# A new order for the first two batches of a fused attention and gated-MLP kernel, with 35 casts and copies on other engines

## The chip, the cores and the metric

The kernel runs on one core of a Trainium2 chip. The core has a matrix engine (PE in the profile, with its weight loads as PEld), a vector engine (DVE), a scalar engine (ACT), a general engine (POOL) and an engine that here only issues transfers (SP). Each works through its own instructions strictly in the order of the program, and they wait for each other through semaphores. Data lie in main memory, in the on-chip memory, and in accumulation banks that PE writes and DVE and ACT read. The metric is the device time of one execution in microseconds (us); lower is better.

## The reference, cut to what matters

```
# q, k, v: [8 batches, 8 heads, 576 tokens, 64]
scores = q @ k^T / sqrt(64)
keep   = (0 <= i - j) and (i - j < 64)          # sliding causal window
attn   = softmax(where(keep, scores, -1e9)) @ v
x = attn, heads side by side                     # [8, 576, 512]

h = relu(x @ w_in)                               # w_in [512, 1024]
u, v = h[..., :512], h[..., 512:]
v_n = (v - mean(v)) / sqrt(var(v) + 1e-6)        # over the last axis
v_s = w_spatial @ v_n + b_spatial                # mixes the 576 tokens
out = (u * v_s) @ w_out                          # w_out [512, 512], float32
```

## The kernel before, in words

The code first makes a list of named steps, each with what it computes and what it needs. One long string, `ORDER`, then says in which order the steps are emitted, on which engine each runs, and which numbered buffer or bank it takes. A word such as `ck1_1:POOL:2` reads: step ck1_1, on POOL, into buffer 2. What stands earlier in the string for the same engine is executed earlier. Nothing else decides the order, and a buffer or bank that is taken again is waited for.

The names follow a scheme. The first digit is the batch (0 to 7). For attention the next is the half g (heads 0 to 3, or 4 to 7), and a third digit u is a pair of heads of that half; `r` in place of them is the last 64 tokens, all heads. For the gated MLP the digit behind the underscore is one of five blocks of tokens (or of features for U and G), and block 4 is the one of 64 tokens.

- `ldq`, `ldk`, `ldv`, `ldwin`, `ldwsp`, `ldwo`, `ldb`: loads, issued by SP in order (L401, L422, L327, L343, L384, L352). A q or k load brings one half (576 KB). A v load brings one block of 128 tokens (128 KB) in 256-byte pieces, five for a half. `ldwin100` to `ldwin111` are the four blocks of w_in for the V product (first digit 1), `ldwin000` to `ldwin011` those for U.
- `cq`, `ck`: casts to 16 bits. `tq`, `tk`: transposes on DVE (L408). `cv`, `sl`, `su`, `s4`: cast of v and copies of it shifted by half a block. `cwin`, `cwsp`, `cwo`, `cb`: casts of the weights. On ACT such a copy is at L293, elsewhere at L301, and long ones on POOL are cut into three at L296.
- `S`: scores on PE (L470, for `r` L539) into two pairs of banks. `E`: exponential on ACT (L477, L549). `M`: the mask, a minimum on DVE (L480, L553). `Z`: sums by a product with ones (L493, L562). `N`, `n`: logarithm and exponential of its negative, which gives the inverse (L519, L521). `P`: product with v (L504, L575). `X`: P times the inverse on DVE (L512, L583), which is x.
- `V`: x times the second half of w_in (L653; block 4 at L666). `Vr`: relu (L633). `Vb`, `Va`: statistics on DVE (L635, L637). `L1`, `L2`: inverse deviation on ACT (L680, L682). `A`: normalisation on DVE (L692). `U`, `Ur`: the other half and its relu (L708, L713, L721).
- `W`: transposes of w_spatial on PE (L368), copied out by `We`. `G`: the spatial product (L738; block 4 at L744). It needs all five A and all five We, and the bias. `Ge`: times u on DVE (L752). `O`, `Oe`, `st`: the output product (L763), its copy on ACT (L610) and the store. From batch 1 on, V of block 4 shares its bank with the output of block 4 of the batch before, so `V1_4` needs w_out and Ge0_4 as well.
- `D`: 25 steps of two products of zeros (L791), which keep PE busy in the first microseconds and compute nothing.

The batches overlap: while the MLP of one batch runs, the attention of the next is computed and the loads of later ones are issued. Loads of q, k and weights go through eight buffers of one kind (`nat`), those of v through four (`natv`); a load into a buffer waits until the casts of what lay there are done.

Of the kernel before, what the change touches and what calls it, by code (L numbers as in the profile page):

```python
# [47 lines left out]
Ge0_4:DVE:1 tq2_0:DVE:3 cv1_11:POOL ldq3_0:DQ:0 G0_1:PE:0 ldv2_00:DQ:0 s41_1:POOL sl1_11:ACT
su1_11:POOL n1_r:ACT Ge0_2:DVE:2 P1_10:PE:2 n1_11:ACT X1_10:DVE:3 ck2_1:POOL:2 P1_11:PE:1
ldk3_0:DQ:2 S2_0:PE:1:0 X1_11:DVE cwo10:ACT ldv2_01:DQ P1_r:PE:2 Ge0_0:DVE:3 V1_2:PE:1 E2_00:ACT:0  # L50
X1_r:DVE:1 Ge0_1:DVE:4 E2_01:ACT:1 V1_1:PE:3 cq2_1:POOL:3 ldv2_02:DQ tk2_1:DVE:0 V1_3:PE:2
Vr1_2:ACT:5 ldv2_03:DQ cwo00:POOL Vr1_1:ACT:6 tq2_1:DVE:1 U1_2:PE:0 ldv2_10:DQ:1 Vr1_3:ACT:7
cwo11:ACT ldv2_11:DQ V1_0:PE:1 M2_00:DVE Ur1_2:ACT:5 Vb1_2:DVE:5 cwo01:ACT S2_1:PE:1:0 Vr1_0:ACT:4
M2_01:DVE Z2_00:PE:3 cq3_0:POOL:0 ldv2_04:DQ E2_10:ACT:3 V1_4:PE:2 Vb1_1:DVE:1 ldv2_12:DQ Va1_2:DVE
Vb1_3:DVE:3 U1_1:PE:0 Vr1_4:ACT:2 M2_10:DVE Oe0_4:ACT:0 O0_0:PE:1 ck3_0:POOL:1 ldv2_13:DQ
Vb1_4:DVE:0 E2_11:ACT:2 Vb1_0:DVE:2 ldq4_0:DQ:3 O0_2:PE:2 Oe0_0:ACT:0 Va1_3:DVE ldv2_14:DQ Va1_4:DVE
Va1_1:DVE Ur1_1:ACT:0 Va1_0:DVE S2_r:PE:1:0 M2_11:DVE Z2_10:PE:1 cv2_00:POOL:1 ldv3_00:DQ:2
L11:ACT:1 O0_1:PE:0 tq3_0:DVE:4 L21:ACT Oe0_2:ACT:1 ldq3_1:DQ:1 N2_10:ACT:3 U1_4:PE:2 ldk3_1:DQ:4
A1_4:DVE E2_r0:ACT:0 U1_0:PE:1 N2_00:ACT:5 A1_0:DVE:4 ldv5_10:DQ:3 A1_2:DVE:5 Ur1_4:ACT:3 A1_1:DVE:6
U1_3:PE:3 Oe0_1:ACT A1_3:DVE:7 sl2_00:ACT:0 su2_00:POOL tk3_0:DVE:5 G1_1:PE:2 Ur1_3:ACT:1  # L60
cv2_10:POOL:0 Ur1_0:ACT:4 G1_0:PE:0 Ge1_1:DVE:5 n2_00:ACT sl2_10:POOL:1 s42_0:ACT Z2_01:PE:3
E2_r1:ACT ldv3_10:DQ:0 Ge1_0:DVE:6 s42_1:ACT P2_00:PE:1 Z2_11:PE:2 su2_10:POOL ldv3_11:DQ
N2_01:ACT:2 S3_0:PE:1:0 X2_00:DVE:0 ldv3_12:DQ N2_11:ACT:4 M2_r:DVE ldq4_1:DQ:7 P2_01:PE:0 n2_10:ACT
cq3_1:POOL:2 P2_10:PE:3 ldv3_13:DQ P2_11:PE:1 n2_11:ACT ldk4_0:DQ:5 X2_10:DVE:1 G1_3:PE:2
E3_00:ACT:0 X2_11:DVE cq4_0:POOL:3 ldv3_01:DQ G1_4:PE:3 n2_01:ACT Ge1_3:DVE:7 O0_3:PE:1 ck3_1:ACT:0
X2_01:DVE Ge1_4:DVE:8 Z2_r:PE:2 V2_2:PE:0 tq3_1:DVE:0 N2_r:ACT:1 E3_01:ACT:1 V2_0:PE:3 M3_01:DVE
V2_3:PE:2 Vr2_0:ACT:3 M3_00:DVE cq4_1:POOL:1 Vr2_2:ACT:1 U2_2:PE:3 tk3_1:DVE:1 Vr2_3:ACT:0 n2_r:ACT
V2_1:PE:0 cv3_10:POOL:2 Oe0_3:ACT Vb2_0:DVE:4 P2_r:PE:2 st0_1:DQ Vr2_1:ACT:2 Z3_00:PE:1 X2_r:DVE:0
S3_1:PE:1:0 sl3_10:POOL:2 st0_4:DQ N3_00:ACT:0 Vb2_3:DVE:5 ldv3_02:DQ U2_0:PE:0 Ur2_2:ACT:2
tq4_1:DVE:2 su3_10:POOL ldv3_03:DQ E3_10:ACT:3 ldv3_14:DQ G1_2:PE:2 ldv3_04:DQ ck4_0:POOL:2  # L70
tq4_0:DVE:3 E3_11:ACT:2 st0_0:DQ Z3_01:PE:1 V2_4:PE:3 Ur2_0:ACT:0 Vb2_1:DVE:3 N3_01:ACT:5 M3_10:DVE
S3_r:PE:1:0 Vr2_4:ACT:4 U2_4:PE:0 Ge1_2:DVE:9 E3_r0:ACT:1 U2_3:PE:1 E3_r1:ACT Va2_0:DVE M3_11:DVE
Ur2_4:ACT:4 cv3_00:POOL:3 Oe1_4:ACT:0 O1_2:PE:2 Vb2_2:DVE:0 n3_01:ACT st1_4:DQ Va2_3:DVE Vb2_4:DVE:1
O1_3:PE:0 n3_00:ACT ldk4_1:DQ:6 sl3_00:POOL:3 ldv4_00:DQ:1 Oe1_2:ACT:1 Va2_4:DVE Va2_2:DVE Va2_1:DVE
U2_1:PE:3 tk4_0:DVE:0 Ur2_3:ACT:1 su3_00:POOL L12:ACT:0 O1_0:PE:2 L22:ACT Oe1_3:ACT A2_4:DVE
s43_0:POOL A2_1:DVE:0 Ur2_1:ACT:3 O1_1:PE:1 ldv4_10:DQ:2 A2_3:DVE:1 s43_1:ACT ldk5_0:DQ:0 A2_0:DVE:2
Oe1_0:ACT:0 Z3_10:PE:0 A2_2:DVE:3 ldv4_11:DQ P3_00:PE:3 N3_10:ACT:3 P3_10:PE:2 ldq5_0:DQ:2
# [764 lines left out]
```

## Time and profile before

| what | value |
|---|---|
| time, median of 3 runs | 202.31 us (201.81 to 206.53) |
| profiled execution, span from first to last instruction | 201.0 us |
| PE busy | 188.6 us, 94% |
| DVE busy | 161.2 us, 80% |
| ACT busy | 167.0 us, 83% |
| POOL busy | 76.5 us, 38% |
| data moved | 42.69 MB, mean 212 GB/s |

The profile gives the profiled execution's time as its span, 201.0 us; the runs' times hold in addition what lies around the span, and their median is 1.3 us above it. Busy PE time counts matmuls as long as they are in the pipeline, so it is not PE at its peak. In the row of a group, the first two numbers are the start and the length in microseconds, xN the number of instructions, and what stands in brackets is the idle time of the engine before it and what ended it. In the chain of work that ended last there is only a start and a length. In a row of transfers the last number is the time from issue to landing.

### The profile page before, as it was taken

How to read it: one execution, taken by the hardware profiler on the slowest of the kernel's cores; microseconds unless marked ns; L12 is line 12 of the kernel's file. 1: busy time of each engine (PE TensorE's matmuls, PEld its weight loads, DVE VectorE, ACT ScalarE, POOL GpSimd, SP SyncE). 2: the span in 40 equal slices, each digit the busy share in tenths (PEclk: the TensorE clock that was granted, in tenths of full speed). 3: DMA queues.
4: the chain of work that ended last, by engine and by line, in shares of the span. 5: the costliest groups of instructions: out<-in, count | busy, mean ns of one | idle time of the engine just before them, and what ended most of it. 6: DMA issues, size and time to landing. Idle time of an engine off the chain costs nothing.

```text
span 201.0 us, 7008 instructions
## 1 busy us (share of the span) xinstructions
PE 188.6 (94%) x2927; PEld 97.7 (49%) x2927; DVE 161.2 (80%) x307; ACT 167.0 (83%) x307; POOL 76.5 (38%) x144
## 2 busy tenths in 40 slices
PE   7588889899999999989999999999999999999992
PEld 2233535545445445654455545554465455444450
...
GB/s 221 387 276 184 336 378 210 292 372 377 185 274 255 246 221 188 295 243 234 311 118 262 241 316 178 227 284 249 185 111 117 3 5 132 108 0 0 128 145 202
DMA packets 50275, 42.69 MB, mean 212 GB/s; under 512 B 39361, under 2 KB 39489, under 8 KB 50242
## 3 DMA queue, kind: packets, MB, share of 16 engines
...
q8 instruction: 23, 0.38, 0.8%
...
q14 instruction: 10, 0.08, 0.1%
...
## 4 chain that ended last, share of the span: by engine, by line
PE 70%; DMA 9%; SPq 7%; ACT 5%; DVE 5%; POOL 1%; issue 1%; POOLq 0%
PE bank L738 16%; PE bank L653 12%; PE bank L763 12%; PE bank L708 10%; DMA nk<-in_k_dram 9%; SPq L422 4%; PE pair L470 4%; PE bank L504 3%; PE bank L666 3%; PE bank L493 3%; PE bank L744 2%; SPq L327 2%; ACT e L477 1%; PE bank L713 1%; ACT ob L610 1%
## 5 line engine op out<-in xcount | busy, mean ns | idle before, releaser
L738 PE MATMUL bank<-wspT,vn 128*128 128x512 f16 (+1 forms) x160 | 37.5, 379 | 0.0
L477 ACT ACTIVATE e<-pair 128x1024 f16<-128x1024 f32 x32 | 31.9, 1027 | 2.7 <-PE pair L470 2.5
L752 DVE TENSOR_TENSOR g<-bank,ru 128x512 f16<-128x512 f32 (+1 forms) x40 | 24.8, 632 | 11.0 <-PE bank L738 5.0
L708 PE MATMUL bank<-x,win 128*128 128x512 f16 x128 | 31.6, 379 | 0.0
L763 PE MATMUL bank<-wout,g 128*128 128x512 f16 x128 | 31.3, 379 | 0.0
L653 PE MATMUL bank<-win,x 128*128 128x512 f16 x128 | 30.4, 379 | 0.2 <-DVE x L512 0.2
L721 ACT ACTIVATE ru<-bank 128x512 f32<-128x512 f32 (+1 forms) x40 | 21.4, 562 | 8.4 <-PE bank L708 4.6
L635 DVE BATCH_NORM_STATS2 st<-vs 128x6 f32<-128x512 f16 (+1 forms) x40 | 25.9, 670 | 3.0 <-ACT vs L633 2.8
L512 DVE TENSOR_TENSOR x<-bank,lz 128x512 f16<-128x512 f32 x32 | 21.2, 683 | 5.4 <-PE bank L504 2.6
L633 ACT ACTIVATE vs<-bank 128x512 f16<-128x512 f32 (+1 forms) x40 | 22.9, 597 | 3.1 <-PE bank L653 2.3
L610 ACT COPY ob<-bank 128x512 f32<-128x512 f32 (+1 forms) x39 | 22.6, 588 | 3.3 <-PE bank L763 3.1
L738 PEld LDWEIGHTS <-vn 128*128 128x128 f16 (+1 forms) x160 | 14.9, 97 | 17.7 <-DVE vn L692 0.5
L480 DVE TENSOR_TENSOR e<-e,mask 128x1024 f16<-128x1024 f16 x32 | 22.5, 721 | 1.0 <-ACT e L477 1.0
L408 DVE STREAM_TRANSPOSE qT<-hq 128x576 f32<-128x576 f32 x16 | 19.7, 1243 | 2.5 <-POOL hq L296 2.3
L296 POOL CAST hq<-nq 128x384 f16<-128x384 f32 x33 | 16.5, 536 | 13.1 <-DMA nq<-in_q_dram 12.5
L408 DVE STREAM_TRANSPOSE kT<-hk 128x576 f32<-128x576 f32 x16 | 20.0, 1247 | 1.4 <-ACT hk L293 1.1
L519 ACT ACTIVATE lz<-bank 128x512 f32<-128x512 f32 x32 | 18.6, 603 | 2.1 <-PE bank L493 2.0
L521 ACT ACTIVATE lz<-lz 128x512 f32<-128x512 f32 x32 | 19.6, 631 | 0.1
L653 PEld LDWEIGHTS <-x 128*128 128x128 f16 x128 | 12.0, 97 | 14.3 <-issue 0.6
L708 PEld LDWEIGHTS <-win 128*128 128x128 f16 x128 | 11.9, 98 | 14.4 <-issue 1.3
L763 PEld LDWEIGHTS <-g 128*128 128x128 f16 x128 | 11.8, 98 | 13.4 <-issue 0.5
L692 DVE TENSOR_SCALAR vn<-vs,mv,ln 128x512 f16<-128x512 f16 (+1 forms) x40 | 15.4, 436 | 3.5 <-ACT ln L682 3.3
...
## 6 DMA issues: line engine op xcount, KB each, us to landing
nq<-in_q_dram SPq DMA_DIRECT2D x16, 576.0 KB, 6.4
nk<-in_k_dram SPq DMA_DIRECT2D x16, 576.0 KB, 5.5
...
wi<-in_moe_w_in_dram SPq DMA_DIRECT2D x8, 256.0 KB, 5.6
...
wo<-in_moe_w_out_dram SPq DMA_DIRECT2D x4, 256.0 KB, 7.1
```

Source lines behind the costliest of these rows:

```text
L408: d = add(f"t{name}{b}_{g}", ("DVE", 1.09), key, lambda e: nc.vector.transpose(qt.t[:, :].rearrange("p (i j) -> p j i", j=18), h.t[:, :].b ...
L477: ex = add(f"E{b}_{g}{u}", ("ACT", 0.91), key, lambda e, u=u: nc.scalar.activation(e2[u].t[:, :, :], sc[u].t[:, :, :], AF.Exp, bias=0.0, s ...
L480: mins.append(add(f"M{b}_{g}{u}", ("DVE", 0.65), key, lambda e, u=u: nc.vector.tensor_tensor(e2[u].t[:, :, :], e2[u].t[:, :, :], mask[:, : ...
L610: lambda e: (nc.vector.tensor_copy if last else nc.scalar.copy)(view(), m.t[rows, 0:n]),
L633: rl = add(f"Vr{b}_{j}", ("ACT", 0.49), key, lambda e: nc.scalar.activation(vs.t[0:jn, :], m.t[0:jn, :], AF.Relu), deps=[pv], acq=[vs], us ...
L635: s1 = add(f"Vb{b}_{j}", ("DVE", 0.6), key + 0.02, lambda e: nc.vector.bn_stats(st6.t[0:jn, 0:6], vs.t[0:jn, :]), deps=[rl], acq=[st6], us ...
L653: nc.tensor.matmul(m.t[:, :], xr(b, r)[:, 128 * j:128 * j + 128], w_in_sb[r][:, 512:1024], start=(r == 0), stop=(r == 3))
L708: nc.tensor.matmul(m.t[:, :], w_in_sb[r][:, 128 * i:128 * i + 128], xr(b, r), start=(r == 0), stop=(r == 3))
L721: lambda e, m=m, ru=ru, n=n: nc.scalar.activation(ru.t[:, 0:n], m.t[:, 0:n], AF.Relu), deps=[pu], acq=[ru], uses=[m])))
L738: nc.tensor.matmul(m.t[:, :], w[0:kn, 128 * i:128 * i + 128], wspT[kk][0:kn, 0:512], start=(kk == 0), stop=(kk == 4))
L752: lambda e, m=m, g=g, ru=ru, n=n: nc.vector.tensor_tensor(g.t[:, 0:n], m.t[:, 0:n], ru.t[:, 0:n], ALU.mult),
L763: nc.tensor.matmul(m.t[:, :], G[r][0].t[:, 128 * j:128 * j + 128], w_out_sb[r][:, :], start=(r == 0), stop=(r == 3))
```

## The change

`ORDER` is another one. No step is added, removed or computed otherwise. What is new in it:

- All steps of batch 0 and most of batch 1 stand in another order. PE keeps the old order for its last 192 of 287 steps, DVE for 196 of 288, ACT for 216 of 307, POOL for 39 of 74, SP for 81 of 155; ahead of that everything moves.
- The k of the first half is loaded ahead of its q. The v loads of half 0 come ahead of those of half 1. `ldk1_1` and `ldq1_1` are ahead of `ldwin000`, the bias load goes behind all w_in, and `ldv1_01` ahead of three of the w_spatial blocks.
- The zero products are in the order of their numbers: 13 ahead of S0_0, 12 up to S1_0, and none behind it (before: 8, 13 and 4).
- S0_r comes ahead of S0_1. V0_4, of 64 tokens, comes ahead of V0_0 to V0_3. Z1_00 goes behind all V0.
- 35 casts and copies change engine. To POOL: ck0_0, ck0_1, cq1_0, ck1_0, su0_00, cv0_01, s40_1, cwin100, cwin000, cwin001, cb, cwsp4, cv1_00, sl1_00, su1_00, sl1_10. To ACT: cq0_0, cq0_1, cv0_00, su0_01, s40_0, sl0_11, cq1_1, We0, We1, cv1_10, cv1_11. To DVE: cwin110, su0_11, cwsp3, cv1_01, s41_0, We3, We4, cwo00.
- Behind that, buffers and banks have other numbers, in the same rotation.

The lines of the string that matter, old and new:

```
-ldq0_0:DQ:0 ldk0_0:DQ:1 D14:PE:0 ldk0_1:DQ:2 ldq0_1:DQ:3 D12:PE:1 ldv0_00:DQ:0 ldq1_0:DQ:4 D23:PE:2
...
-ldv0_14:DQ Z0_00:PE:1 E0_r0:ACT:0 cv0_10:DVE:0 Z0_10:PE:2 E0_r1:ACT M0_11:DVE ldwin110:DQ:7
...
-ldwin101:DQ D8:PE:1 su0_01:DVE sl0_01:POOL n0_10:ACT su0_10:DVE D13:PE:2 ldwin000:DQ:1 n0_01:ACT
-tk1_0:DVE:5 s40_0:POOL ldk1_1:DQ:2 N0_11:ACT:4 P0_01:PE:3 ldq1_1:DQ:3 P0_00:PE:1 n0_11:ACT
...
-n0_r:ACT X0_11:DVE cwin000:ACT Z1_00:PE:1 M1_01:DVE ldwsp1:DQ:6 P0_r:PE:0 cb:ACT V0_1:PE:3
-X0_r:DVE:0 V0_2:PE:2 ck1_1:POOL:2 ldwsp4:DQ:0 Vr0_1:ACT:0 N1_00:ACT:5 Vb0_1:DVE:0 V0_0:PE:0
-Vr0_2:ACT:1 tk1_1:DVE:0 cq1_1:POOL:3 ldv1_00:DQ:2 V0_3:PE:3 Vr0_0:ACT:2 n1_00:ACT ldwsp0:DQ:2
-Z1_01:PE:1 tq1_1:DVE:1 V0_4:PE:2 cwin001:ACT cwin010:POOL ldv1_01:DQ N1_01:ACT:2 cwin011:POOL
-Vr0_3:ACT:3 ldv1_02:DQ Vb0_2:DVE:1 S1_1:PE:0:1 Vr0_4:ACT:4 Vb0_0:DVE:2 cwsp3:POOL ldv1_03:DQ
-U0_2:PE:0 E1_11:ACT:2 Vb0_3:DVE:3 cwsp2:POOL ldv1_04:DQ U0_3:PE:1 Va0_2:DVE Va0_3:DVE E1_10:ACT:3
...
-A0_1:DVE:3 N1_r:ACT:0 We1:DVE ck2_0:POOL:0 ldwo10:DQ:5 P1_00:PE:0 Z1_10:PE:3 X1_00:DVE:2 G0_4:PE:2
...
+ldk0_0:DQ:0 D0:PE:0 D1:PE:1 D2:PE:2 D3:PE:3 ck0_0:POOL:0 tk0_0:DVE:0 D4:PE:0 ldq0_0:DQ:1
...
+N0_01:ACT:2 ldwin110:DQ:6 ldv0_14:DQ ldwin100:DQ:7 ldwin111:DQ ldwin101:DQ M0_10:DVE su0_00:POOL
+sl0_01:POOL D20:PE:0 s40_0:ACT D21:PE:2 D22:PE:0 n0_00:ACT n0_01:ACT D23:PE:2 ldk1_1:DQ:0
+su0_10:DVE M0_11:DVE cv0_11:DVE sl0_11:ACT su0_11:DVE ldq1_1:DQ:1 s40_1:POOL cwin100:POOL
+ldwin000:DQ:2 D24:PE:0 S1_0:PE:0:1 ldwin010:DQ:3 ldwin011:DQ Z0_10:PE:2 P0_00:PE:1 P0_01:PE:0
+n0_r:ACT Z0_11:PE:3 N0_10:ACT:3 N0_11:ACT:4 n0_10:ACT n0_11:ACT X0_00:DVE:0 X0_01:DVE E1_01:ACT:0
+P0_r:PE:1 cwin110:DVE X0_r:DVE:0 P0_10:PE:2 cwin111:POOL cwin101:POOL P0_11:PE:0 V0_4:PE:3
+ldwin001:DQ ldwsp4:DQ:4 ldb:DQ:5 Vr0_4:ACT:0 X0_10:DVE:1 X0_11:DVE V0_0:PE:1 V0_1:PE:2
+ldv1_00:DQ:2 V0_2:PE:0 M1_01:DVE cq1_1:ACT:2 ck1_1:POOL:3 tk1_1:DVE:0 tq1_1:DVE:1 E1_00:ACT:1
+V0_3:PE:3 M1_00:DVE Vr0_0:ACT:1 Vr0_1:ACT:2 Vb0_1:DVE:0 Vr0_2:ACT:3 Z1_00:PE:1 ldv1_01:DQ
+cwin000:POOL cwin010:POOL Vr0_3:ACT:4 Vb0_2:DVE:1 S1_1:PE:1:0 cwin011:POOL ldwsp2:DQ:6 ldwsp3:DQ:7
...
+E1_10:ACT:2 E1_11:ACT:3 Va0_4:DVE Va0_0:DVE Va0_3:DVE U0_1:PE:2 ldq2_0:DQ:2 Ur0_1:ACT:0 U0_4:PE:0
+U0_3:PE:3 U0_0:PE:1 L10:ACT:0 Ur0_3:ACT:1 Z1_01:PE:2 S1_r:PE:1:0 M1_10:DVE M1_11:DVE L20:ACT
+Ur0_4:ACT:2 ldv1_12:DQ ldv1_13:DQ cwsp3:DVE A0_1:DVE:0 A0_0:DVE:1 Ur0_0:ACT:3 Z1_11:PE:3
+Z1_10:PE:0 N1_01:ACT:0 cv1_00:POOL:2 sl1_00:POOL:2 N1_11:ACT:2 E1_r0:ACT:1 ldv1_14:DQ cwsp0:DVE
+N1_10:ACT:1 U0_2:PE:1 A0_4:DVE A0_3:DVE:2 E1_r1:ACT cv1_01:DVE M1_r:DVE cwsp2:POOL cb:POOL
+A0_2:DVE:3 cwsp1:POOL W0:PE:2 W1:PE:3 ldq2_1:DQ:4 W4:PE:0 Ur0_2:ACT:4 We1:ACT We4:DVE W2:PE:1
+su1_00:POOL s41_0:DVE n1_00:ACT We0:ACT n1_01:ACT cv1_10:ACT:3 n1_11:ACT W3:PE:3 We2:DVE We3:DVE
+ldk2_1:DQ:6 sl1_01:POOL su1_01:POOL P1_00:PE:0 P1_01:PE:1 Z1_r:PE:2 G0_4:PE:3 ldv2_00:DQ:0
...
+su1_11:POOL cq2_1:POOL:3 P1_10:PE:0 P1_11:PE:2 tq2_0:DVE:3 S2_0:PE:1:0 E2_01:ACT:1 E2_00:ACT:0
+Ge0_3:DVE:2 ck2_1:POOL:2 X1_10:DVE:3 X1_11:DVE tq2_1:DVE:0 G0_0:PE:1 Ge0_0:DVE:3 V1_2:PE:0
+Vr1_2:ACT:5 V1_1:PE:2 V1_3:PE:1 Vr1_1:ACT:6 U1_2:PE:0 n1_r:ACT Vr1_3:ACT:7 V1_0:PE:2 cwo10:ACT
+Ur1_2:ACT:5 P1_r:PE:1 Ge0_2:DVE:4 M2_00:DVE Vb1_2:DVE:5 tk2_1:DVE:1 X1_r:DVE:1 S2_1:PE:0:1
+ldq3_0:DQ:1 cwo00:DVE cwo11:ACT cwo01:ACT Vr1_0:ACT:2 M2_01:DVE Z2_00:PE:3 E2_10:ACT:2 V1_4:PE:0
...
```

More of the change, by code (lines that the diff above doesn't have):

```diff
@@ L48 @@
[L48 to L77, printed above, removed]
@@ new lines @@
+ck0_1:POOL:3 D14:PE:2 D15:PE:3 tk0_1:DVE:3 D16:PE:0 D17:PE:1 S0_r:PE:0:1 D18:PE:2 E0_r0:ACT:0
+E0_r1:ACT ldv0_00:DQ:0 ldv0_01:DQ ldk1_0:DQ:5 ldv0_02:DQ ldv0_03:DQ M0_01:DVE M0_00:DVE Z0_01:PE:3
+cq1_0:POOL:0 cv0_00:ACT:0 M0_r:DVE tq1_0:DVE:4 sl0_00:DVE:0 ck1_0:POOL:1 Z0_00:PE:0 S0_1:PE:0:1
+Z0_r:PE:1 D19:PE:2 N0_00:ACT:0 tk1_0:DVE:5 E0_10:ACT:2 E0_11:ACT:3 cv0_01:POOL ldv0_10:DQ:1
+ldv0_11:DQ ldv0_04:DQ ldv0_12:DQ ldv0_13:DQ cv0_10:DVE:1 sl0_10:DVE:1 su0_01:ACT N0_r:ACT:1
+N0_01:ACT:2 ldwin110:DQ:6 ldv0_14:DQ ldwin100:DQ:7 ldwin111:DQ ldwin101:DQ M0_10:DVE su0_00:POOL
@@ new lines @@
+N2_10:ACT:4 U1_4:PE:0 A1_4:DVE E2_r0:ACT:0 U1_0:PE:2 N2_00:ACT:5 A1_0:DVE:4 A1_2:DVE:5 Ur1_4:ACT:0
+A1_1:DVE:6 U1_3:PE:3 Oe0_1:ACT A1_3:DVE:7 G1_1:PE:0 cv2_00:POOL:0 sl2_00:ACT:0 ck3_0:POOL:0
+tk3_0:DVE:4 cq3_0:POOL:1 tq3_0:DVE:5 su2_00:POOL Ur1_3:ACT:1 Ur1_0:ACT:3 G1_0:PE:1 Ge1_1:DVE:5
+n2_00:ACT Z2_01:PE:3 E2_r1:ACT Ge1_0:DVE:6 Z2_11:PE:2 N2_01:ACT:0 S3_0:PE:0:1 N2_11:ACT:1 M2_r:DVE
+s42_0:ACT P2_00:PE:0 X2_00:DVE:0 P2_01:PE:1 n2_10:ACT ldv2_10:DQ:1 ldv2_11:DQ ldv2_12:DQ
+ldv2_13:DQ ldv2_14:DQ cv2_10:POOL:1 ldq3_1:DQ:3 ldk3_1:DQ:2 sl2_10:POOL:1 s42_1:ACT su2_10:POOL
@@ new lines @@
+P2_10:PE:3 cq3_1:POOL:3 P2_11:PE:2 ldv3_00:DQ:2 n2_11:ACT ldk4_0:DQ:4 X2_10:DVE:1 ldq4_0:DQ:6
+G1_3:PE:0 ldv5_10:DQ:3 E3_00:ACT:0 X2_11:DVE cq4_0:POOL:2 ldv3_10:DQ:0 ldv3_11:DQ ldv3_12:DQ
+ldv3_13:DQ ldv3_01:DQ G1_4:PE:3 n2_01:ACT Ge1_3:DVE:7 O0_3:PE:2 ck3_1:ACT:0 ldq4_1:DQ:5 X2_01:DVE
+Ge1_4:DVE:8 Z2_r:PE:0 V2_2:PE:1 tq3_1:DVE:0 N2_r:ACT:2 E3_01:ACT:1 V2_0:PE:3 M3_01:DVE V2_3:PE:0
+Vr2_0:ACT:0 M3_00:DVE cq4_1:POOL:1 Vr2_2:ACT:4 U2_2:PE:3 tk3_1:DVE:1 Vr2_3:ACT:3 n2_r:ACT
+V2_1:PE:1 cv3_10:POOL:2 Oe0_3:ACT Vb2_0:DVE:4 P2_r:PE:0 st0_1:DQ Vr2_1:ACT:1 Z3_00:PE:2 X2_r:DVE:0
@@ L147 @@
+Oe7_0:ACT:0 st7_0:DQ O7_3:PE:3 Oe7_1:ACT st7_1:DQ O7_4:PE:0 Oe7_3:ACT st7_3:ACT Oe7_4:DVE:0
+st7_40:DQ st7_41:ACT
 """
```

175 lines of the change are left out of this document (88 added, 87 removed).

## The prediction

> **What bounds the kernel now.** I read the page's first line, then the chain that ended last, then the busy time by stretches, cut where the chain changes hands.
>
> ```profile
> span 201.0 us, 7008 instructions
> ```
> ```profile
> core 0: us, PE busy (x) PEld busy (x) DVE busy (x) ACT busy (x) POOL busy (x), PEclk, DMA share, GB/s
> 15.00:19.00 4.00, 3.43 (x54) 1.31 (x52) 3.92 (x12) 3.35 (x8) 0.71 (x2) 1.00 0.68 166
> 24.60:39.90 15.30, 13.92 (x220) 7.51 (x216) 13.91 (x31) 13.94 (x29) 9.77 (x17) 1.00 1.02 298
> 39.90:201.00 161.10, 155.83 (x2352) 81.19 (x2351) 127.02 (x235) 136.59 (x256) 59.33 (x108) 0.99 0.66 194
> ```
>
> From 39.9 us on PE is busy 155.8 of 161.1 us, and PE's sum of work there is not touched by the change. So the kernel is a head of 39.9 us that ends when the first spatial product (G0_4) can start, and a tail of 161.1 us that PE paces. What the change is worth is the time by which G0_4 moves, plus what the changed order costs in the few microseconds behind it. The chain says what sets G0_4:
>
> ```profile
> 19.27 6.71 DMA nk<-in_k_dram
> ...
> 26.10 1.41 POOL hk L296 x3
> 27.51 1.39 POOL hq L296 x3
> ...
> 28.92 1.27 DVE qT L408
> ...
> 30.23 0.81 PE pair L470 x46
> ...
> 31.07 1.94 ACT e L477 x2
> ...
> 38.25 1.12 DVE vn L692 x2
> ...
> 39.42 0.46 DVE wspT L301
> ...
> 39.91 0.76 PE bank L744 x20
> ...
> 51.24 0.70 PE pair L470 x51
> ```
>
> The reader is to see a relay: the load ldk1_1 lands at 19.27 + 6.71 = 25.98, POOL casts k and then q of batch 1's second half one behind the other, DVE transposes, PE scores (S1_1, 30.23), ACT exponentiates, and then ACT and DVE work through the normalisation of batch 0 and the spatial weights until We1 ends at 39.88. From the landing of k1_1 to G0_4 it is 13.9 us. PE is not the bound there (13.92 busy in 15.30).
>
> **The change part by part.** No instruction of work is added. Up to the second transpose nothing is gained: k and q of half 0 change places in the load queue and casts change engines (POOL 1.41 for ACT's 1.15), but the first scores need both, and the second landing goes through the shorter cast as before. S0_1 slips behind the 64-token scores S0_r, about 1.3 us; this is free, since it ends well before V0 can start, as follows.
>
> V0, the first product with w_in, starts when the last of the four w_in loads of that half is cast, and the loads come late:
>
> ```profile
> 4.63 8.55 SPq L422 DMA_DIRECT2D nv<-in_v_dram  x6
> ...
> 18.27 0.42 SPq L327 DMA_DIRECT2D wi<-in_moe_w_in_dram  x1
> wi<-in_moe_w_in_dram SPq DMA_DIRECT2D x1, 256.0 KB, 5.6
> 19.74 0.38 SPq L401 DMA_DIRECT2D nq<-in_q_dram  x1
> nq<-in_q_dram SPq DMA_DIRECT2D x1, 576.0 KB, 7.7
> ```
>
> ldwin101 lands at 18.27 + 5.6 = 23.9 and ldq1_1 at 19.74 + 7.7 = 27.4. In the new order the same loads stand ahead of ldwin101, except the bias; ahead of ldq1_1 the bias and ldwin000 are gone. At 298 GB/s the 256 KB of ldwin000 are 0.9 us. So ldq1_1 lands at 26.5 if the queue flows as before. It could flow better: from 15 to 19 the queue moved 166 GB/s, behind v loads that SP issues slowly (six of them took 8.55 us, row 4.63); at 298 those 0.66 MB would take 2.2 us, 1.8 less, which gives 24.7. No row shows the new interleaving of v and q, k. Bounds 24.7 and 27.4 (no gain at all); I take 26.2, nearest to the 26.5 of an unchanged flow, since the same v loads still stand in front.
>
> This landing, t, is what decides, because cq1_1 goes from POOL to ACT, whose queue is in order: behind it wait E1_00, the four Vr0 and all that follows up to We1 and We0 (moved here from DVE). The terms:
>
> ```profile
> 41.39 1.15 ACT L293 CAST hq<-nq 128x1152 f16<-128x1152 f32 x1
> 31.07 1.94 ACT L477 ACTIVATE e<-pair 128x1024 f16<-128x1024 f32 x2 [0.43 <-PE pair L470]
> 26.88 1.14 ACT L633 ACTIVATE vs<-bank 128x512 f16<-128x512 f32 x2
> 33.14 1.06 ACT L721 ACTIVATE ru<-bank 128x512 f32<-128x512 f32 x2
> 35.22 0.41 ACT L721 ACTIVATE ru<-bank 128x256 f32<-128x256 f32 x1
> 35.48 0.63 ACT L519 ACTIVATE lz<-bank 128x512 f32<-128x512 f32 x1
> 32.94 0.30 ACT L680 ACTIVATE ln<-mv,eps_t 128x5 f32<-128x5 f32 x1
> 34.09 0.20 ACT L682 ACTIVATE ln<-ln 128x5 f32<-128x5 f32 x1
> 34.69 0.66 ACT L549 ACTIVATE er<-pair 128x256 f16<-128x256 f32 x2
> 37.24 1.16 ACT L293 COPY wspT<-bank 128x576 f16<-128x576 f16 x2
> ```
>
> cq1_1 1.15; three E1 1.94 x 1.5 = 2.91; four Vr0 2.28; N1_00, N1_01, N1_11, N1_10 4 x 0.63 = 2.52; Ur0_1, Ur0_3, Ur0_0, Ur0_2 2.12, Ur0_4 0.41; L10 and L20 0.50; E1_r0 and E1_r1 0.66; We1 and We0 1.16; n1_00 as long as an N, 0.63. Together 14.3. Neighbours overlap by about 0.1 (the group at 33.14 ends at 34.20, and the next starts at 34.09); of the 23 joints some 8 lie inside the pairs above, so 15 x 0.1 = 1.5 comes off: 12.8. Then We0's bank goes to Z1_r, and G0_4 follows it: 0.3 with the hand-offs, an estimate. So G0_4 starts at t + 13.1 if ACT never waits.
>
> Does it wait? PE has the same products in this stretch as before, and it idled 1.4 us of the 15.3 then, so it waits for ACT more than ACT for it. DVE ends on the same clock: M1_r needs E1_r1, which ACT ends 3 us before We0; behind it stand A0_2, We4, s41_0, We2, We3, at 0.56 for vn (38.25) and 0.46 for a copy (39.42) some 2.4, so We3 ends within half a microsecond of We0. The cover is thin on both, and I add nothing. The spatial weights land last in this stretch in both orders; the new one puts ldv1_01 ahead of the last of them, 0.13 MB or 0.4 us at 298 GB/s, and they move with ldq1_1 otherwise, so W0 (behind N1_01, about t + 9.5) gets no later condition than before unless the queue slips.
>
> With t = 26.2, G0_4 starts at 39.3: 0.6 earlier. With 24.7 it is 37.8, 2.1 earlier; with 27.4, 40.5, 0.6 later. Break-even is 26.8.
>
> V0_4 first needs X0_r alone of batch 0's attention, but it needs all four w_in casts too, and ldwin101 is the later condition; so V0 starts when it did, or with the loads a little sooner. Behind the five products PE stands at Z1_00, whose mask M1_00 is now behind tq1_1 on DVE (t + 1.2 + 1.3 + 0.7 = 29.4). Before, S1_1 stood at 30.23 in the same way. What an earlier V0 would gain is lost there.
>
> Behind G0_4 three edits count against the change. G0_0 goes behind S2_0, P1_r behind V1_0, tk2_1 behind tq2_1, two Ge0, M2_00 and Vb1_2 on DVE. S2_1 waits for tk2_1, and DVE from We3 to there is about 11 us of unbroken work by the rows above (transposes at 1.27, the rest near 0.6); PE took 11.3 to there before (39.91 to 51.24). I add 0.2. cwo00 on DVE stands just ahead of M2_01, and V1_4 waits for it beside cwo01 on ACT, which is as late. tq3_0 moves behind the A1: S3_0, which needs it, stands behind four U1, O0_1 and two G1 on PE, and these hide it; without them it is one transpose, 1.3 us.
>
> ```profile
> 57.48 5.84 SPq L422 DMA_DIRECT2D nv<-in_v_dram  x4
> ...
> 66.64 0.43 SPq L422 DMA_DIRECT2D nv<-in_v_dram  x1
> 71.41 0.39 SPq L626 DMA_DIRECT2D out_dram<-ob  x1
> ```
>
> The loads of batches 2 to 4 change places on SP, and s42_0, whose end frees the buffer of ldv3_10, goes behind N2_01 and N2_11 on ACT, 1.2 us later. SP's idle time hides this: from 67.07 it waits 4.3 us for the first store.
>
> Sum: -0.6 + 0.2 = -0.4 on the execution's 201.0, so a span of 200.6. The runs' median is 202.31, 1.3 above that span (their lowest 0.8 above); the same difference gives 201.9.
>
> **DVE and POOL in each other's way.** Sixteen casts and copies come to POOL and ten leave it. The same instruction has two prices in this trace:
>
> ```profile
> 22.36 1.15 DVE L480 TENSOR_TENSOR e<-e,mask 128x1024 f16<-128x1024 f16 x1
> 24.62 0.68 DVE L480 TENSOR_TENSOR e<-e,mask 128x1024 f16<-128x1024 f16 x1
> 32.08 0.67 POOL L301 CAST wnat<-ws 128x576 f16<-128x576 f32 x1 [0.26 <-DMA ws<-in_moe_w_spatial_dram]
> 33.19 1.42 POOL L301 CAST wnat<-ws 128x576 f16<-128x576 f32 x1 [0.44 <-DMA ws<-in_moe_w_spatial_dram]
> ```
>
> The slow mask ran while POOL cast w_in, the slow cast while DVE did masks: 0.47 and 0.75 lost. The Trainium skill, page "SBUF — State Buffer", section "Who interferes with whom", says that a DVE instruction with two SBUF inputs and a GpSimd one that reads SBUF exclude each other, so that the second waits for the whole of the first; the trace agrees with these two pairs, and by that rule the change, which brings POOL more work, pays for it. In the stretch that decides, DVE is as long as ACT, so a collision there counts: two or three more of 0.5 us make 1.0 to 1.5. I hold this as a rival, not as a term, because the old stretch has POOL busy for 9.8 of 15.3 us already.
>
> **The rivals.** (1) The loads flow freely: t = 24.7, -2.1 + 0.2, so 200.4. For it: 298 GB/s right behind the slow stretch. Against: SP still issues ten v loads.
>
> (2) Slower, by ACT's queue: ldq1_1 lands late, and every microsecond behind 26.8 holds all of ACT for one. It decides from there: t = 28.5 gives +1.9, 204.2, and over 2% needs t above 30.6. For it: row 4.63, SP held up for 8.55 us by v loads, and six of the ten now follow one another without q or k between. Against: between ldk1_0 and ldk1_1 stand eight v and four w_in loads, where nine and five stood.
>
> (3) The collisions above: +1.2 on the forecast, 203.1.
>
> (4) PE's clock. The warm-up products that stood between P0 and V0 are now all ahead of S1_0, so PE idles from P0_11, which by way of P0_r and s40_1 waits for the last v load, to V0_4, which waits for ldwin101, three loads later. Three times 256 KB are 2.6 us at 298 GB/s and 4.7 at 166; the P products and the casts take about 1 of it.
>
> ```profile
> 1.27 5.35 PE L791 MATMUL bank<-scratch 128*128 128x512 f16 x16 [1.27 <-DVE scratch L234]
> 8.67 0.76 PE L470 MATMUL pair<-qT,kT 32*64 32x128 f16 x64 [2.05 <-DVE kT L408]
> 9.37 1.90 PE L791 MATMUL bank<-scratch 128*128 128x512 f16 x8
> ```
>
> Sixteen products from a cold start took 5.35, eight after a gap of 2.05 took 1.90: the gap did not cool PE, the cold start cost 5.35 - 3.80 = 1.6. A gap of 1.6 to 3.7 may; then V0 runs up to 1.6 longer, of which the wait at Z1_00 hides about 1.2 and in the worst case none: +0.4 to +1.6, 202.3 to 203.5. The Trainium skill, page "TensorE: Matmul & The Clock Gate", section "Why this matters for your kernels", asks for no PE gaps above about 3 us; by that rule the new gap lies at the border, and the trace shows only that 2.05 is harmless.
>
> **How the numbers follow.** Forecast (t between 25.4 and 27.4, 201.1 to 203.1): 0.52. Rival 1: 0.17; 2: 0.13; 3: 0.10; 4: 0.08. Two per cent, 4 us here, is about what a measurement of this kernel can tell from no change, and it lies at 198.3 and 206.4. Rival 1 would have to be doubled to get there: 0.04 faster. Rival 2 past 30.6 and sums of 2, 3 and 4: 0.06 slower. The rest, 0.90, within. The range takes in the floor of rival 1 and reaches, above, to 204.2, which is rival 2 at 28.5; both unknown costs (the landing, the collisions) have their ends inside.
>
> **What would show it.** Right: G0_4 at 39.3, within 0.8; cq1_1 on ACT ending an idle time of ACT at about 26; S1_1 near 30; PE continuous from G0_4 to S2_1; the tail 161 us. Wrong: an ACT that never waits for q1_1 (then t was not the bound and DVE or a cast is); a V0 at half rate; a tail that differs from 161 us by over a microsecond, which would mean that the order behind batch 1 matters and I had called it free.

## The result, and the profile after

The changed kernel takes 204.47 us (median of 4 runs, 203.55 to 205.65). The kernel before, run beside it, takes 202.06 us. The ratio is 1.0126, with a 95% interval of 1.0083 to 1.0168: 1.3% slower, inside the two per cent, above the forecast of 201.9 and 0.3 above the 204.2 to which the range reaches. A ratio here leaves out executions that are more than 1.5% above the shortest of their kernel; of e6 below that leaves two of six, its profile is of one of the other four (207.40 us), and its median over all six is 2.4% above the kernel before.

The page's first line and the same stretches as before, the second cut at the new start of G0_4 (columns: stretch, length, busy time and instructions of each engine, granted clock of PE, share of the transfer engines, GB/s). The last stretch shown is new:

```profile
span 201.8 us, 7019 instructions
```
```profile
core 0: us, PE busy (x) PEld busy (x) DVE busy (x) ACT busy (x) POOL busy (x), PEclk, DMA share, GB/s
15.00:19.00 4.00, 3.73 (x85) 2.04 (x83) 3.18 (x7) 3.93 (x7) 2.13 (x4) 1.00 0.75 188
24.60:40.44 15.84, 14.53 (x215) 7.21 (x214) 14.54 (x30) 14.28 (x27) 11.39 (x19) 0.93 1.10 304
40.44:201.80 161.36, 156.03 (x2355) 81.25 (x2352) 130.03 (x236) 136.78 (x256) 57.67 (x106) 1.00 0.65 191
23.50:27.00 3.50, 3.50 (x9) 1.06 (x8) 2.06 (x3) 2.55 (x4) 1.78 (x3) 0.51 1.01 365
```

The head is 40.44 us instead of 39.91, the tail 161.36 instead of 161.10. That is 0.8 us in all, while the medians differ by 2.4: what lies around a span is about 1.75 us in these runs (203.55 for the span of 201.8), so the median runs have spans near 202.7 and 200.3; the profile of the changed kernel is of its shortest run, 0.9 below, and the one of before is 0.7 above. So one pair of profiles tells where to look, and the size has to come from many runs. Between 23.5 and 27 PE had half its clock.

The chain of work that ended last (start, length):

```profile
19.82 4.20 DMA nk<-in_k_dram
24.15 1.79 POOL hk L299 x3
25.96 1.26 DVE kT L411
27.22 1.08 DVE qT L411
28.30 0.55 DVE e L483
...
34.37 0.84 DVE wnat L304
35.21 1.09 DVE vn L695 x2
36.48 0.44 DVE wnat L304
...
39.46 0.45 DVE wspT L304
...
40.50 0.71 PE bank L747 x20
...
51.54 0.69 PE pair L473 x52
...
72.67 0.96 POOL hq L299 x2
...
82.70 0.40 POOL hs L304
83.12 0.37 SPq L425
...
91.00 5.02 DMA nk<-in_k_dram
96.59 0.96 POOL hk L299 x2
...
103.21 0.30 PE bank L565 x4
```

Before, the head's chain went over POOL's two casts, DVE, PE and ACT. Now it starts with ldk1_1 and POOL's cast of it and runs down DVE from 25.96 on, nearly alone, to the last We. ACT waited only 0.22 us for q1_1 in this execution, so here the landing of ldq1_1, the prediction's t, is not what set G0_4. And in the tail a long relay has come in: POOL's casts of batch 4 from 72.67 on, a v buffer they free at 82.70, the loads behind it, a k load, POOL again, PE at 103.21.

The timeline of the changed kernel where the chain changes hands (start, length, instruction; in brackets the idle time before it and what ended it), ACT, DVE and PE of the head first, then SP, POOL and PE of the tail:

```profile
25.48 1.15 ACT L296 CAST hq<-nq 128x1152 f16<-128x1152 f32 x1 [0.22 <-DMA nq<-in_q_dram]
...
38.01 0.64 ACT L296 COPY wspT<-bank 128x576 f16<-128x576 f16 x1 [1.00 <-PE bank L371]
...
39.07 0.63 ACT L296 COPY wspT<-bank 128x576 f16<-128x576 f16 x1
...
32.10 2.27 DVE L483 TENSOR_TENSOR e<-e,mask 128x1024 f16<-128x1024 f16 x2
...
36.98 2.40 PE L371 MATMUL bank<-id,wnat 128*128 128x128 f16 x25 [0.96 <-DVE wnat L304]
...
57.96 9.52 SPq L425 DMA_DIRECT2D nv<-in_v_dram  x6
67.52 0.50 SPq L404 DMA_DIRECT2D nq<-in_q_dram  x1
71.90 0.39 SPq L629 DMA_DIRECT2D out_dram<-ob  x1
...
72.22 1.41 POOL L299 CAST hq<-nq 128x384 f16<-128x384 f32 x3 [6.13 <-DMA nq<-in_q_dram]
...
100.41 1.02 PE L711 MATMUL bank<-x,win 128*128 128x512 f16 x4 [0.69 <-ACT vs L636]
...
103.21 0.30 PE L565 MATMUL bank<-er,ones 128*64 128x128 f16 x4 [0.45 <-DVE er L556]
```

The reader is to see two things. In the head, cwsp0 on DVE (ends 36.92) lets W0 start at 36.98, after PE stood for 0.96 us, and so ACT stands for 1.00 before We1. In the tail, ldq4_1 is issued at 67.52 behind six v loads, the second of which waits for the buffer that s42_0 frees. The kernel before had here, by its timeline of SP, POOL and PE:

```profile
63.37 1.77 SPq L401 DMA_DIRECT2D nq<-in_q_dram  x1
...
69.81 1.41 POOL L296 CAST hq<-nq 128x384 f16<-128x384 f32 x3 [3.10 <-DMA nq<-in_q_dram]
...
87.44 0.30 PE L562 MATMUL bank<-er,ones 128*64 128x128 f16 x4 [0.56 <-DVE g L752]
```

The load went 4.15 us sooner and its cast 2.41, and PE stood for 0.56 us at Z3_r, where now it stands for 0.69 at U3_1 and 0.45 at Z4_r. SP still idles for 3.9 us ahead of the store at 71.90; POOL idles for 6.13 where it idled for 3.10, and the steps behind it are late. Over the whole tail PE is idle for 5.33 us (161.36 less 156.03) where it was idle for 5.27 (161.10 less 155.83): this one pair shows the places, and not yet a loss.

### The profile page after: what moved, and what is told of

It is laid out like the page before. It is cut to its first block, busy times and chain, and to the rows that moved or that the text cites. A ratio compares the mean times of both kernels' runs of the same rounds, so it can differ in the third digit from the quotient of the medians.

```text
span 201.8 us, 7019 instructions
## 1 busy us (share of the span) xinstructions
PE 191.7 (95%) x2927; PEld 98.5 (49%) x2927; DVE 163.0 (81%) x302; ACT 167.1 (83%) x306; POOL 81.8 (41%) x154
## 4 chain that ended last, share of the span: by engine, by line
PE 61%; SPq 13%; DVE 8%; POOL 7%; DMA 5%; ACT 3%; issue 2%; POOLq 0%
PE bank L741 15%; PE bank L766 11%; PE bank L656 10%; PE bank L711 8%; SPq L425 8%; DMA nk<-in_k_dram 5%; PE bank L507 3%; SPq L404 3%; PE pair L473 3%; PE bank L496 2%; POOL hk L299 2%; PE bank L747 2%; PE bank L669 2%; POOL hs L302 2%; DVE st L638 2%
## 5 line engine op out<-in xcount | busy, mean ns | idle before, releaser
L656 PE MATMUL bank<-win,x 128*128 128x512 f16 x128 | 31.6, 390 | 0.0
L299 POOL CAST hk<-nk 128x384 f16<-128x384 f32 x36 | 18.6, 551 | 16.8 <-DMA nk<-in_k_dram 10.0
L483 DVE TENSOR_TENSOR e<-e,mask 128x1024 f16<-128x1024 f16 x32 | 23.9, 764 | 1.1 <-ACT e L480 0.7
L299 POOL CAST hq<-nq 128x384 f16<-128x384 f32 x30 | 15.1, 540 | 11.8 <-DMA nq<-in_q_dram 9.4
L695 DVE TENSOR_SCALAR vn<-vs,mv,ln 128x512 f16<-128x512 f16 (+1 forms) x40 | 17.1, 477 | 3.3 <-ACT ln L685 3.1
```

Source lines behind the costliest of these rows:

```text
L299: nc.gpsimd.tensor_copy(o[:, n:n + 384], i[:, n:n + 384])
L483: mins.append(add(f"M{b}_{g}{u}", ("DVE", 0.65), key, lambda e, u=u: nc.vector.tensor_tensor(e2[u].t[:, :, :], e2[u].t[:, :, :], mask[:, : ...
L656: nc.tensor.matmul(m.t[:, :], xr(b, r)[:, 128 * j:128 * j + 128], w_in_sb[r][:, 512:1024], start=(r == 0), stop=(r == 3))
```

## The experiments

Theory A has two parts. (a) The far part of the new order costs most of the loss: s42_0 ends later, it frees the buffer of ldv3_10, and ldq4_1 is queued behind that load and its followers. (b) The head costs the rest, since ACT and DVE need longer from the landing of ldq1_1 to G0_4 than the prediction's sum. Rivals: collisions of DVE and POOL, PE's clock, or no cost in the far part at all. All ratios are to the kernel before; behind each stand 6 or 12 runs of the variant and 17 to 37 of the kernel before. In the variants the lines carry the numbers of the kernel before (three less). The edits are words of `ORDER`.

**e1: the changed kernel again.**

> The changed kernel once more, without an edit, for the spread of its executions and a second profile. Its first profiled execution had a span of 201.8 us, the shortest of four (201.8 to 203.9). Theory T (tail): the time is lost behind batch 2, by loads that come late, and the amount differs from execution to execution; then the median ratio stays near 1.012, and a profile of a slower execution has the same first G0_4 (about 40.4 us) and more PE idle time behind 85 us than the 1.1 us of the first one. Theory H (head): the loss is made before the first G0_4, which then moves with the time of the execution, and the tail is a constant.

Measured: 205.14 us, ratio 1.0137 (1.0085 to 1.0188). Its profile, timeline of ACT and PE:

```profile
27.56 1.15 ACT L296 CAST hq<-nq 128x1152 f16<-128x1152 f32 x1 [2.34 <-DMA nq<-in_q_dram]
...
30.80 0.41 PE L496 MATMUL bank<-e,ones 128*64 128x512 f16 x2 [2.64 <-DVE e L483]
...
42.20 0.77 PE L747 MATMUL bank<-wspT,vn 128*128 128x64 f16 x20
```

The same program, but ldq1_1 lands 2.1 us later, ACT stands for 2.34 us until it does, PE stands for 2.64 at Z1_00, and G0_4 starts at 42.20 instead of 40.44. Of the 2.4 us by which this span is longer, 1.8 lie ahead of G0_4 and 0.6 behind it. So the landing varies from execution to execution by most of the 2.7 us between my bounds, and here it does hold ACT, and through E1_00 and M1_00 also PE.

**e2: ldq4_1 early.**

```
 G1_3:PE:0
+ldq4_1:DQ:5
 ldv5_10:DQ:3
...
 ck3_1:ACT:0
-ldq4_1:DQ:5
 X2_01:DVE
```

> One word moved in the changed order: the load ldq4_1 goes ahead of ldv5_10, so that it no longer stands behind five v loads that wait for s42_0. Theory T: cq4_1 starts about 67 us instead of 72.2, POOL's copies of v for batch 3 and 4 follow 2 to 3 us sooner, the v buffers come free sooner, and the PE idle time behind 85 us falls; 0.8 to 2 us less than the changed kernel, so 1.002 to 1.008 of the kernel before. Theory H: no difference beyond 0.3 us; 1.012.

Measured: 203.32 us, ratio 1.0048 (1.0019 to 1.0077). The timeline of SP and POOL:

```profile
58.43 1.05 SPq L401 DMA_DIRECT2D nq<-in_q_dram  x2
...
68.64 1.41 POOL L296 CAST hq<-nq 128x384 f16<-128x384 f32 x3 [0.30 <-DVE x L512]
```

ldq4_1 is now the second of the pair at 58.43, POOL no longer waits for it, and behind G0_4 PE has no idle time that the timeline shows. One load moved in the queue gives back 0.9% of the 1.4%. The profiles of the other variants agree in the place: PE stands at U3_1 in all six executions with ldq4_1 late (the changed kernel 0.69, e1 0.75, e3 1.10, e4 0.64, e6 0.65, e9 1.35 us) and in none of the six with the new head and ldq4_1 early (e2, e5, e7, e10, e11, e12). From G0_4 to the end it is 161.4 to 162.1 us in the changed kernel, e1, e3 and e4 (mean 161.8), and 160.1 to 161.4 in those six with the load early, three of which also have s42_0 back (mean 160.6). That is 1.2 us, less than the 1.8 that the times give.

**e9: s42_0 back, ldq4_1 left late.** The other end of the same chain.

```
 n2_00:ACT
+s42_0:ACT
 Z2_01:PE:3
...
 M2_r:DVE
-s42_0:ACT
 P2_00:PE:0
```

> The changed kernel with one word moved: s42_0 directly behind n2_00 on ACT, its place in the kernel before; ldq4_1 stays late in SP's queue. Theory A (the late s42_0 holds the v loads of batch 3 and through them ldq4_1 behind them): s42_0 at about 61.9 instead of 63.6, ldq4_1 and cq4_1 1.5 to 2 us sooner than in the changed kernel, no gap of PE or under 0.3 us at U3_1 and Z4_r, ratio 1.003 to 1.007. Rival B (the place of ldq4_1 behind these loads is enough by itself): the gaps at U3_1 and Z4_r stay, ratio 1.011 to 1.014 as for the changed kernel.

Measured: 203.68 us, ratio 1.0048 (1.0014 to 1.0083), the same gain as e2. Its profile does not show the gain. It is of an execution of 205.59 us, the third longest of twelve. The timeline of SP and PE:

```profile
59.50 2.33 SPq L401 DMA_DIRECT2D nq<-in_q_dram  x1
61.93 7.42 SPq L422 DMA_DIRECT2D nv<-in_v_dram  x6
69.40 0.50 SPq L401 DMA_DIRECT2D nq<-in_q_dram  x1
...
102.96 1.02 PE L708 MATMUL bank<-x,win 128*128 128x512 f16 x4 [1.35 <-ACT vs L633]
```

There SP was held for 2.33 us at ldq4_0 (row 59.50), ahead of the six v loads, so ldq4_1 went at 69.40, 1.88 later than in the changed kernel, and the gap at U3_1 is still there. By the list of SP's waits, 2.1 us of that were spent waiting for POOL. That s42_0 is a link of the chain rests on the times alone.

**e6: the far part alone, in the kernel before.**

```
 sl2_10:POOL:1
-s42_0:ACT
 Z2_01:PE:3
...
 Ge1_0:DVE:6
-s42_1:ACT
 P2_00:PE:1
...
 N2_11:ACT:4
+s42_0:ACT
 M2_r:DVE
-ldq4_1:DQ:7
 P2_01:PE:0
 n2_10:ACT
+s42_1:ACT
...
 ldv3_01:DQ
+ldq4_1:DQ:7
 G1_4:PE:3
```

> The kernel before with only the far part of the change: ldq4_1 behind ldv3_01 on SP's queue, s42_0 behind N2_11 and s42_1 behind n2_10; batches 0 and 1 stay as they were. Theory A (the loads of batches 3 and 4 behind the late s42_0 cost about 1.8 us): G0_4 stays at 39.9, ldq4_1 lands near 72, cq4_1 comes some 2 us later, gaps of PE show at U3_1 or Z4_r, ratio 1.007 to 1.010. Rival B (the prediction's step, that this order is free): ratio 0.999 to 1.001.

Measured: ratio 1.0112 (1.0041 to 1.0182). The timeline of SP, POOL, DVE and PE:

```profile
69.21 0.50 SPq L401 DMA_DIRECT2D nq<-in_q_dram  x1
...
75.66 1.41 POOL L296 CAST hq<-nq 128x384 f16<-128x384 f32 x3 [7.89 <-DMA nq<-in_q_dram]
...
77.10 2.34 DVE L408 STREAM_TRANSPOSE qT<-hq 128x576 f32<-128x576 f32 x2 [2.56 <-POOL hq L296]
...
81.62 1.89 PE L763 MATMUL bank<-wout,g 128*128 128x512 f16 x8 [2.37 <-DVE g L752]
...
103.82 1.02 PE L708 MATMUL bank<-x,win 128*128 128x512 f16 x4 [0.65 <-ACT vs L633]
```

The same picture without the new head: POOL idles for 7.89 us and the gap opens at U3_1. The delay is larger than expected (cq4_1 5.9 us late, where about 2 were expected); a part of it is not the edit's, since G0_4 of this execution, at 40.92, is itself 1.0 late. The rows at 77.10 and 81.62 show a second way from the late load to PE, which theory A does not have: the transpose tq4_1 stands in DVE's list, DVE idles for 2.56 us until q4_1 is cast, Ge1_2 behind it is late, and PE stands for 2.37 us at O1_2. In the other profiles with the load late this way costs little: PE stands there for 0.18 us in e1, 0.33 in e3, 0.43 in e9 and not at all in the changed kernel. That the far part costs is shown from both sides, by e2 and e6; how the cost divides between the two ways is not.

**e8: ldq4_1 early in the kernel before.** It goes ahead of `ldv5_10:DQ:3`, as in e2.

> The kernel before with only ldq4_1 issued earlier, ahead of ldv5_10. Theory A (in the kernel before, the loads of batch 4 are in time but for one gap of PE of 0.56 us at Z3_r, which another load sets): ratio 0.997 to 1.000. Rival B (the queue behind ldq4_1 still sets part of the tail): POOL's casts of batch 4 come some 1 to 2 us sooner and the ratio is 0.993 to 0.996.

Measured: ratio 1.0003 (0.9967 to 1.0039). In the kernel before the load had enough room; more of it gives nothing that these runs can tell. Its one profile is of the longest of its twelve executions (204.60 us), and there PE stands for 0.51 us at U3_1 and 0.82 at Z4_r with ldq4_1 early: five v loads from 83.27 on took 7.33 us to issue, and the k load behind them went at 90.65, where in the profile of the kernel before it went at 88.66. So these two places can be hit in another way too.

**e10: head alone.** The edits of e2 and e9 together.

> The changed kernel with both moves: ldq4_1 ahead of ldv5_10 and s42_0 directly behind n2_00. What is left of the change is the new order of batches 0 and 1. Theory A (head and far part add up: 1.0137 less the 1.0112 of the far part alone, and 1.0048 with ldq4_1 early): ratio 1.002 to 1.005, G0_4 0.5 to 1.6 us late depending on the landing of ldq1_1. Rival B (the head itself costs nothing, the rest of the far part does it): ratio 0.999 to 1.001.

Measured: 203.45 us, ratio 1.0022 (0.9992 to 1.0052), G0_4 at 40.74. By itself this does not exclude that the head is free. But e2, e9 and e11 (below) have the same head, one load aside, and none of the four is under 1.002: their mean is 1.0041, or 0.8 us, if either link mended is enough.

**e3: one cast less on POOL, one more on ACT.** It tells a collision from a long list on ACT: cb took 1.01 us on POOL beside DVE's masks and normalisations.

```
 cwsp2:POOL
-cb:POOL
 A0_2:DVE:3
...
 Ur0_2:ACT:4
+cb:ACT
 We1:ACT
```

> The cast of the bias, cb, goes from POOL to ACT, behind Ur0_2, where ACT stood idle for 1.0 us; POOL's copies then run 1 us less beside DVE's A0_1 and A0_0, which took 0.74 each instead of 0.40. Theory H with DVE and POOL in each other's way: A0_1 and A0_0 at 0.40, the first G0_4 0.5 to 0.8 us sooner (39.7 to 39.9), and the time less by the same. Theory T: G0_4 sooner all the same, but the time less by 0.3 at most, since the loads behind batch 2 set the end.

Measured: 206.39 us, ratio 1.0188 (1.0134 to 1.0243). Not faster; by the middle values 1 us slower than e1 on the same chip, though the intervals touch. In its profile PE waits for We1 on ACT:

```profile
40.58 0.52 PE L368 MATMUL bank<-id,wnat 128*128 128x128 f16 x5 [0.84 <-ACT wspT L293]
```

Taking work from POOL did not pay here, and in this execution ACT's list is on the path. What the move of cb costs is not shown: q1_1 landed late in this execution (cq1_1 at 27.67), and G0_4, at 41.99, is 14.3 us behind that, no longer than the 14.6 of e1.

**e4: the clock of PE.** Four of the zero products go where PE idled, into bank 3.

```
-D21:PE:2 D22:PE:0 ... D23:PE:2 ... D24:PE:0
...
 n0_r:ACT
+D21:PE:3 D22:PE:3
 Z0_11:PE:3
...
 P0_11:PE:0
+D23:PE:3 D24:PE:3
 V0_4:PE:3
```

> Four of the products of zeros go from ahead of S1_0 to the gap before V0: two ahead of Z0_11, two ahead of V0_4, so that PE's clock stays granted in full. In the changed kernel the clock was halved from 23.5 to 26.9 us and the five V0 took 1.85 us longer. If that were on the path: 1.0 to 1.8 us less. By the prediction's walk Z1_00 behind them waits for a mask that is ready at 28.85, only 0.4 before V0 ends, and U0_1 for the cast of ldwin001 at 30.8: 0 to 0.4 us less. Theory T: 0 to 0.4 as well.

Measured: 204.93 us, ratio 1.0122 (1.0072 to 1.0172), no difference from e1. The stretch that had half a clock, and PE behind V0:

```profile
23.50:27.00 3.50, 3.50 (x17) 1.45 (x16) 2.01 (x4) 2.12 (x4) 1.95 (x4) 1.00 1.05 387
```
```profile
28.76 0.41 PE L493 MATMUL bank<-e,ones 128*64 128x512 f16 x2 [1.16 <-DVE e L480]
```

The clock stays full and PE does 17 products where it did 9. In this execution the time won is spent at Z1_00, where PE now waits 1.16 us for the mask M1_00. In e1 the slow clock comes later and has a part in the head: it is at 0.50 between 32 and 35, behind the pause of 2.64 us, and ACT stands for products of U0:

```profile
35.88 0.60 ACT L724 ACTIVATE ru<-bank 128x512 f32<-128x512 f32 x1 [1.31 <-PE bank L711]
```

**e5: E1_00 and M1_00 earlier,** on top of e2: E1_00 directly behind E1_01 on ACT, M1_00 directly behind M1_01 on DVE. **e7:** e5 with cwsp0 directly behind cwsp3 on DVE, and the zero products of e4. **e12:** e7 with s42_0 as in e9.

> The changed kernel with ldq4_1 issued ahead of ldv5_10, E1_00 put directly behind E1_01 on ACT (ahead of Vr0_4 and cq1_1), and M1_00 directly behind M1_01 on DVE (ahead of tk1_1). Theory A (the head's loss is the order in which ACT and DVE take up their work around the landing of ldq1_1): G0_4 comes 0.6 to 0.9 us sooner after that landing than with the loads alone (about 13.4 us behind it instead of 14.1), PE no longer waits long for M1_00 at Z1_00, and the ratio to the kernel before falls from 1.005 to 1.000 to 1.002. Rival B (collisions of DVE and POOL, or the landing times alone, set it): G0_4 stays 14 to 15 us behind the landing, ratio 1.004 to 1.006 as with the loads alone.

> The kernel of e5_E1_early with two more moves: cwsp0 directly behind cwsp3 on DVE, and the filler matmuls D21 to D24 ahead of Z0_11 and V0_4 as in e4_warm. Theory A (order of ACT, DVE and PE in the head): another 0.3 to 0.8 us off G0_4, since W0 no longer waits for cwsp0 and V0 runs at the full clock; ratio 0.996 to 0.999. Rival B (once one list is shorter the next is as long): the same as e5_E1_early, within 0.2%.

> The kernel of e7_three with s42_0 directly behind n2_00: all moves that a profile spoke for together. Theory A (each gives back its part): ratio 0.998 to 1.001, at best level with the kernel before, because G0_4 cannot come sooner than the lists of ACT and DVE behind the landing of ldq1_1 let it. Rival B (the 64-token product first has a gain that the lost time hid): ratio below 0.996.

Measured: e5 1.0056 (1.0025 to 1.0087), e7 1.0029 (0.9991 to 1.0066), e12 1.0037 (1.0006 to 1.0069). The profiles move as theory A says: G0_4 comes 13.7 us behind the start of cq1_1 in e5, and at 40.01 in e12. The times do not. By the middle values they lie within 0.2% of e2 and e10, and the intervals, 0.3 to 0.4% to either side, leave room for a small gain only; the sizes that theory A gave to these moves were missed in e5 and e7, and that of e12 lies at the edge of its interval. No version beats the kernel before.

**e11: ldq1_1 one place later.** On top of e10, behind `ldwin000:DQ:2`.

> The kernel of e10_head_alone with ldq1_1 one place later in SP's queue, behind ldwin000, so that q1_1 lands some 0.7 to 1.5 us later: the price of the landing. Theory A (ACT's list starts at this landing and G0_4 hangs on it nearly 1:1): ratio 0.003 to 0.007 above e10_head_alone. Rival B (DVE's list without a gap is the bound, the landing hides behind it): within 0.002 of e10_head_alone.

Measured: ratio 1.0046 (1.0014 to 1.0078), 0.0024 above e10 with intervals that overlap. In the execution profiled the load was not late at all (cq1_1 at 25.78). It settles nothing.

## Why the prediction was wrong, step by step

**"SP's idle time hides this" (the loads of batches 2 to 4, put at nothing): the step that failed most.** I took the cover from the wrong engine. SP did idle for 4 us before the store, and still does. But the cover of a load is the time until its data are wanted, and POOL wanted q4_1 as soon as its earlier casts were done: before, it had already stood for 3.10 us when that load landed. A load 4 us later is a cast 2.4 us later here, and POOL is a queue: the casts of v free the buffers for the next loads, and behind a k load that follows these PE stands. DVE is a second such queue, with tq4_1 in it, as e6 shows. e2, e9 and e6 price it at 0.9%, 0.9% and 1.1%, about 1.8 to 2.2 us. The prediction had s42_0's delay, as 1.2 us (it is 2.2 in the profile: 63.60 for 61.36, of which 0.3 to 0.5 come with the head, by S2_1 and G0_4), and it had the buffer that it frees. It did not follow the queue behind that buffer to its last load.

**G0_4 = t + 13.1.** Five executions have the same head as the changed kernel. Start of cq1_1 (t) and start of G0_4, from their timelines:

| kernel | cq1_1 | G0_4 | difference |
|---|---|---|---|
| after | 25.48 | 40.44 | 14.96 |
| e10 | 26.15 | 40.74 | 14.59 |
| e2 | 27.42 | 41.53 | 14.11 |
| e1 | 27.56 | 42.20 | 14.64 |
| e9 | 27.78 | 41.38 | 13.60 |

At the t that I took, G0_4 is at 40.74 and not at 39.3: the term is 1.4 us short. The sum over ACT's instructions was good. In the changed kernel ACT goes from 25.48 to 39.70, the end of We0, in 14.22 us, of which 1.27 are idle (0.27, and the 1.00 before We1); the other 12.95 stand against 12.8. What failed is "if ACT never waits", with "the cover is thin on both, and I add nothing": ACT waits for PE, PE for cwsp0, and cwsp0 for a DVE that is busy without a pause from 25.96 on (the chain above stays on it). The last 0.3 was 0.74: DVE's copies of w_spatial end at 40.26, 0.56 behind We0, and PE still runs P1_01 and Z1_r before G0_4. The differences are smaller on the whole where t is later; that fits a DVE that sets the early cases and an ACT with a larger part in the late ones, but no run shows it.

**The landing, t = 26.2, bounds 24.7 to 27.4.** A fair middle: the mean of the five is 26.9. But the prediction treated it as one unknown number, and it is another one in each execution. With e3, e4, e5, e7 and e12, which have the same loads ahead of it, cq1_1 starts at 25.48, 25.74, 25.82, 25.83 and 26.15, or at 27.42, 27.43, 27.56, 27.67 and 27.78: two groups, with nothing between (at 26.15, in e10, the load was no longer waited for). Why there are two stays open. The mean lies just past the break-even of 26.8, so even with the right sum the head would have won nothing. The mean of the five G0_4 is 41.26, against 40.23 in three executions with the old head (39.91, e8 39.87, e6 40.92): 1.0 us late in the profiles, and 0.4 to 1.0 in the times of e10, e2 and e9. Forecast was 0.6 early. Which of ACT, DVE, the collisions and the landing has how much of this stays open.

**Behind G0_4, +0.2.** S2_1 starts at 51.54, 0.30 later than before, with G0_4 0.53 later: nothing was lost there. A small miss on the other side.

**V0 and Z1_00.** Right in the place: PE stands at Z1_00 for M1_00 in e1 and e4, and S1_1 was near 30. The start of V0 was not "as before": V0_4 began at 22.43 and waited again for a w_in cast. In the changed kernel's profile V0 then ran at half a clock, between 23.5 and 27.

**The rivals.** (1), free loads, did not come; t never fell under 25.4. (2), the late q1_1, came in three of the five executions, with ACT standing for 2.34 us in e1. (3): the collisions are there (two masks in 2.27 us in the row at 32.10, where one alone took 0.68). The Trainium skill, page "SBUF — State Buffer", section "Who interferes with whom", says that a DVE instruction with two SBUF inputs contends with a GpSimd one that reads SBUF; the trace agrees, as POOL casts and copies from 31.80 to 34.89 while the two masks run from 32.10 to 34.37. Their size is near what this rival named: the same five instructions on DVE (the two masks, cwsp3, A0_1 and A0_0) take 4.46 us in the changed kernel, from 32.10 to 36.56, and 2.98 in e3, from 34.18 to 37.16, so DVE is 1.5 us longer there, on the chain of the profile shown. e3, with cb on ACT, won nothing, but it does not exclude this rival: its landing was late, ACT had more to do, and a cast of w_spatial on POOL took 1.78 us there, at 34.55, beside the same masks. What the collisions cost with an early landing stays open. (4): the clock did fall, by a way not foreseen; in e4 a wait of 1.16 us at Z1_00 takes the place of the slow products and the time stays, so in that execution the cover of about 1.2 us that the prediction saw there was real. In e1 the clock fell later, under U0, where ACT stands for it.

**The signs named.** The tail of the profile shown differs from 161 us by only 0.4, and by the prediction's own test (over a microsecond) the order behind batch 1 would be free. It is not. With one profile of each kernel the test was too coarse for executions whose landings vary by 2 us. SP's idle time, which the prediction took for the cover, never could have shown it. Of the other signs, a V0 at half rate came, and an ACT that never waits for q1_1 nearly did: in that profile it waits for 0.22 us, so there the landing was not the bound.

**What follows for the size.** Far part 1.8 to 2.2 us and head 0.4 to 1.0 make 2.2 to 3.2; measured were 2.4 (204.47 less 202.06) and, in e1, 2.7.
